# Column sums of phi(k) from operand sums, z placed later, and reciprocals by Ln and Exp in a two-block linear-attention kernel

## The chip, the cores and the metric

The kernel runs on one core of a Trainium2 chip. The metric is the device time of one execution in microseconds (us). Three runs of the kernel before gave 188.87, 189.10 and 189.14 us, median 189.1. The profile is of one further execution.

## The reference

```python
def _A_ref(x, wqkv, wo):                  # B=1, S=2048, D=640; _B_ref is the same function
    H = 32; Dh = D // H                   # 32 heads of 20
    q, k, v = ...                         # (x @ wqkv), split by kind and head
    phi = lambda t: jnp.where(t > 0, t + 1, jnp.exp(t)) + 1e-6
    pq, pk = phi(q), phi(k)
    kv = jnp.einsum("bhsd,bhse->bhde", pk, v)
    z = jnp.einsum("bhsd->bhd", pk)       # column sums of phi(k)
    num = jnp.einsum("bhqd,bhde->bhqe", pq, kv)
    den = jnp.einsum("bhqd,bhd->bhq", pq, z)[..., None] + 1e-6
    return merge_heads(num / den) @ wo

x = A_x
g = sigmoid((x * gate_w).sum(-1, keepdims=True))
a = _A_ref(x, A_wqkv, A_wo)
b = _B_ref(x, B_wqkv, B_wo)               # called on the same x
return g * a + (1 - g) * b
```

All arrays are bf16. Each token therefore needs, per head, one factor g/den for block A and (1-g)/den for block B.

## The kernel before

The 2048 tokens are 16 tiles of 128 (ST = 16, hc = 8 is half of them); the 640 features are 5 strips of 128 (DT = 5) or two halves of 320 (HF). `xn` holds x with tokens on partitions, `xT` with features on partitions. `pk` is phi(k) with tokens on partitions, `pqT[b]` is phi(q) with features on partitions, its features ordered so that partition p of strip m is feature 5p + m (`mixed`).

Instead of v, the kernel forms G = x^T phi(k), 640 by 640 (`GT`), then the per-head blocks of wv^T G, then M = (those blocks) wo. The output is the sum over both blocks of (scaled phi(q)) M.

**Stages, in PE's order.** k chunks and the first half of q of block A; then the second half of q (`q_pass`, five `q_unit`s, each two runs of five matmuls of 512 columns); then G of block A: the fifth strip of x plainly (`g_pass`, 32 matmuls of 320 columns), the other four strips by one level of Strassen's scheme (`g_strassen`, seven products of 16 matmuls, line 488). Block B's k and q follow, woven together (`q_strassen`), with M of A among them and after them (`m_block`, line 902). Then G of B in the same way (`g_pass`, `g_strassen`), M of B, and the output products over both blocks.

**Operand sums.** Strassen's scheme needs sums of quarters of x (`x_sum`, into `SX[1..4]`, VectorE, 128x2048) and of phi(k) (`k_sum`, into `TK[b][1..4]`, VectorE, 128x2560). b11, b12 are the first eight token tiles of phi(k), left and right half of the columns; b21, b22 are the last eight. All go through `add_rows` (line 627). For x transposed and wq the same is done by `sq_sum` and `tq_sums`; `p_diff` and `p_sums` make operands of the output products.

**The normalisation.** `z_rows` (line 551) multiplies a 128x32 block of ones with every token tile of `pk`: 16 tiles by two column halves, four tiles at a time on four 32-column strips of the PE array, and masks the result so that row h keeps only the 20 columns of head h (`zr`, line 556). `z_pass` (line 566) turns `zr` to features on partitions and adds the four strips, five matmuls of 32 columns, copied to `zsel` (line 570). `rec_pass` multiplies `zsel` with `pqT[b]` (line 203, 40 matmuls on 32-column strips): den, 32 heads by 4 token groups on partitions, 512 columns. Line 617 adds EPS and multiplies with the gate's factor `ge`, line 622 takes the reciprocal on VectorE. `norm_spread` (line 664) copies each head's row to its four partitions by eight matmuls of 32 rows, ScalarE writes `R` (line 669), and `scale` (line 677) multiplies `pqT[b]` with it.

The gate's logit comes as one more column of the first block's k product; `gl` is its Exp, `gate_rows` makes 1/g and 1/(1-g) of it (`gf`), `gate_spread` transposes them on PE (line 223), copies them (line 225) and sends them through DRAM to `ge` on SP's queue.

**What sets the order.** Under `manual_schedule` every engine executes its instructions in the order in which the program writes them; semaphores hold an instruction until its operands and its place are free. PSUM has four slots of two banks: `ps(name)` takes the next in turn, `ps(name, slot)` a named one, and a new tile in a slot waits for the last reader of the old one. So in `q_pass` the order is: unit 0, `z_rows`, `gate_spread`, then units with `x_sum` and `k_sum` in front of their phi on VectorE, `z_pass` after unit 2. In block B it is `g_pass` with two `m_block`s inside, `m_block` 2 and 3, `z_rows`, `m_block` 4 and 5, the reload of M through DRAM and the load of wo on SP, then `g_strassen` with `z_pass` in its first product.

Of the kernel before, what the change touches and what calls it, by code (L numbers as in the profile page):

```python
# [1 line left out]

# [6 lines left out]
P = 128  # L9
# [7 lines left out]
DT = D // P  # L17
# [7 lines left out]
NG = 8  # L25
K6 = 120
EPS = 1e-6
RB = 256
SH = S // 2

# [2 lines left out]
def kernel(  # L33
# [63 lines left out]
    spread = persist.tile([P, P], BF16, name="spread")  # L97
    R = persist.tile([P, 2, 4, RB], BF16, name="R")
    lift = persist.tile([P, 1], FP32, name="lift")
    ones = persist.tile([P, H], BF16, name="ones")  # L100
    g5 = persist.tile([DT, P], BF16, name="g5")
    gl = persist.tile([P, ST], FP32, name="gl")
# [30 lines left out]
    nc.vector.memset(ones[:], 1.0)  # L133
    nc.vector.memset(KVT[:], 0.0)
    nc.vector.memset(lift[:], 1.0 + EPS)
    xb0 = x2[0:CB * P, :].rearrange("(p q) d -> p q d", q=CB)
    wk = [None, None]
    wv = [None, None]
# [13 lines left out]
    load_x(nc.scalar, 2, 3)  # L152
    load_wk(nc.sync, 2, 3)
    load_x(nc.scalar, 3, 4)
    load_wk(nc.sync, 3, DT)
    wq[0] = wpool.tile([P, DT, D], BF16, tag="wq", name="wqA")
    for lo, hi in ((0, 2), (2, 4), (4, DT)):
# [166 lines left out]
    def mixed(t, m):  # L324

        return t[:, m::DT]
# [13 lines left out]
    def q_unit(b, m, h, lifted=False, slot=None, between=None):  # L340

        pt = ps(f"q{'AB'[b]}", slot)
        q_two(b, [(m, 2 * h), (m, 2 * h + 1)], pt)
        phi(pqT[b][:, m, h * 2 * HB:(h + 1) * 2 * HB].rearrange("p (b n) -> p b n", b=2), pt, lifted, between)

    def q_block(b, m, n, between=None):
# [100 lines left out]
    def g_pass(b, c, slot, between=None):  # L447

        pt = ps(f"g{'AB'[b]}", slot)
        for i in range(ST):  # L450
            if between is not None and i == ST // 2:
# [41 lines left out]
    def g_strassen(b, select, second, spare):  # L493

        x11, x12 = [xn[:, k:k + hc, 0:ic] for k in (0, hc)]
        x22 = xn[:, hc:ST, ic:2 * ic]
        b11 = pk[:, 0:hc, 0:HF]
        b21, b22 = [pk[:, hc:ST, n * HF:(n + 1) * HF] for n in range(2)]
        lo, hi = GT

        def temp(name):
            return work.tile([P, 2, HF], FP32, tag="osb", name=name, bufs=3)

        def add(dst, pt, sb):
# [5 lines left out]
        nc.scalar.copy(out=odd[:, :, 0:HF], in_=even[:, :, 0:HF])  # L510
        if b == 1:
# [4 lines left out]
        u2 = temp("u2")  # L516
        nc.scalar.copy(out=u2[:], in_=odd[:, :, 0:HF])
        if b == 1:
            k_sum(1, 4)
        g_prod(even, x12, b21, False)  # L520
        nc.scalar.copy(out=lo[:, 0:2, :], in_=even[:, :, 0:HF])
        if b == 0:
            k_sum(0, 4)
# [12 lines left out]
        scale(b, 2)  # L536
        scale(b, 3)
        g_prod(odd, x22, TK[b][4], False)
        nc.scalar.copy(out=lo[:, 2:4, :], in_=odd[:, :, 0:HF])
        scale(b, 4)  # L540
        g_prod(even, SX[4], b22, False)
        for n in range(2):
            nc.vector.tensor_tensor(out=hi[:, n, :], in0=even[:, n, 0:HF], in1=u2[:, n], op=ALU.add)

    def z_rows(b, slot=None):

        pt = ps(f"z{'AB'[b]}", slot)
        for k in range(ST // 4):
            for hf in range(2):
                for j in range(4):  # L550
                    nc.tensor.matmul(
                        pt[32 * j:32 * j + 32, hf, 0:HF], lhsT=ones[:], rhs=pk[:, 4 * k + j, hf * HF:(hf + 1) * HF],
                        start=(k == 0), stop=(k == ST // 4 - 1), tile_position=(0, 32 * j),
                    )
# [5 lines left out]
        return zr  # L560

    def z_pass(b, zr, slot=None):

        pt = ps(f"zs{'AB'[b]}", slot)
        for c in range(DT):
            nc.tensor.matmul(
                pt[:, 0, c * H:(c + 1) * H], lhsT=mixed(zr[:], c), rhs=I4[:], start=True, stop=True,
            )
        zsel = work.tile([P, DT, H], BF16, tag="zsel", name="zsel", bufs=1)
        nc.vector.tensor_copy(out=zsel[:], in_=pt[:, 0, 0:DT * H].rearrange("p (c h) -> p c h", h=H))  # L570
        return zsel

    def kvt_mm(b, pt, at, hf):
# [34 lines left out]
    def rec_pass(b, zsel, slot):  # L608

        pt = ps(f"den{'AB'[b]}", slot)  # L610
        for h in range(2):
            by_group(pt[:, 0, h * RB:(h + 1) * RB], zsel, pqT[b], h)
        rts = []
        for h in range(2):
            part = slice(h * RB, (h + 1) * RB)
            d1 = work.tile([P, RB], FP32, tag="d1", name="d1")
            nc.vector.scalar_tensor_tensor(
                out=d1[:], in0=pt[:, 0, part], scalar=EPS, in1=ge[:, b, part], op0=ALU.add, op1=ALU.mult
            )
            rT = work.tile([P, RB], BF16, tag="rT", name="rT")  # L620
            with nc.allow_low_precision(reason="a fp32 reciprocal, stored as the bf16 that multiplies bf16"):
                nc.vector.reciprocal(out=rT[:], in_=d1[:])
            rts.append(rT)
        return rts

# [152 lines left out]
    def q_pass(units):  # L778

        units = list(units)  # L780
        q_unit(0, *units.pop(0))
        zr = z_rows(0)
        gate_spread()
        for k in range(2):
            x_sum(1 + k)
            q_unit(0, *units.pop(0), True)
        zsel = z_pass(0, zr)
        for k, (m, h) in enumerate(units):
            if k < 2:
                if k:  # L790
                    x_sum(3)
                else:
                    k_sum(0, 2)
            q_unit(0, m, h, True)
        sq_sum(4, 0)
        return zsel

    with tc.manual_schedule():
        k_first()
# [19 lines left out]
    with tc.manual_schedule():  # L819
# [12 lines left out]
        g_strassen(0, lambda: zsel, 1, 3)  # L832

        tq_sums(1)
        new_stage("weave")
# [206 lines left out]
```

## Time and profile before

| What | us |
| --- | --- |
| median of three runs | 189.1 |
| the profiled execution | 189.34 |
| its span, first to last instruction | 187.6 |
| 38.5 to 58.3, second half of q, `g_pass` and first product of block A: PE / VectorE / ScalarE busy | 19.67 / 18.76 / 11.12 of 19.80 |
| 58.3 to 73.0, rest of `g_strassen` of A | 14.70 / 14.42 / 5.28 of 14.70 |
| 117.0 to 133.0, `g_pass` of B to `norm_spread` | 15.99 / 15.62 / 8.06 of 16.00 |
| 133.0 to 142.0, rest of `g_strassen` of B | 9.00 / 8.60 / 3.67 of 9.00 |

The profile names an instruction by its line, its engine, and out<-in with shapes. PE is TensorE's matmul and PEld its load of the stationary operand, which normally runs under the matmul before; `128*40` is such an operand of 128 rows and 40 columns, and `128x40` after it is the output. DVE is VectorE, ACT ScalarE, SP the queue that issues most DMA. A matmul's duration goes from its start to the arrival of its last column, so consecutive matmuls overlap; what one costs is the distance between starts. The chain of waits goes back from the last instruction, at each step to what released it; it is printed in order of time as start, length, what. Its times are those in which that link set the end.

The four reciprocals (line 622) take 1753 ns each, the column sums (line 551) 300 ns a matmul with four running side by side, and the table load of ScalarE (line 212) 1283 ns, once, at 2.69 us.

### The profile page before, as it was taken

How to read it: one execution, taken by the hardware profiler on the slowest of the kernel's cores; microseconds unless marked ns; L12 is line 12 of the kernel's file. 1: busy time of each engine (PE TensorE's matmuls, PEld its weight loads, DVE VectorE, ACT ScalarE, POOL GpSimd, SP SyncE). 2: the span in 40 equal slices, each digit the busy share in tenths (PEclk: the TensorE clock that was granted, in tenths of full speed). 3: DMA queues.
4: the chain of work that ended last, by engine and by line, in shares of the span. 5: the costliest groups of instructions: out<-in, count | busy, mean ns of one | idle time of the engine just before them, and what ended most of it. 6: DMA issues, size and time to landing. Idle time of an engine off the chain costs nothing.

```text
span 187.6 us, 3635 instructions
## 1 busy us (share of the span) xinstructions
PE 182.6 (97%) x1447; PEld 122.5 (65%) x1456; DVE 155.8 (83%) x268; ACT 87.0 (46%) x150; POOL 9.1 (5%) x25
## 2 busy tenths in 40 slices
PE   8899999999999999999999999999999999999993
PEld 3666657765577677676666655767677776777772
DVE  1468868889999999998898987999997989787554
ACT  2065488545842432455868686662611611111110
POOL 8920000000000000000000000000000000000000
PEclk9999999999999999999999999999999999999999
DMA  5996449984250000005000000145600003312222
GB/s 181 277 171 86 101 98 302 349 205 152 56 178 0 0 3 0 0 3 175 0 0 5 0 0 0 34 141 198 159 0 0 3 0 104 109 70 71 73 72 70
DMA packets 19769, 16.18 MB, mean 86 GB/s; under 512 B 8968, under 2 KB 19624, under 8 KB 19752
## 3 DMA queue, kind: packets, MB, share of 16 engines
q1 hardware_dynamic: 18888, 15.13, 29.3%
q10 hardware_dynamic: 864, 0.82, 1.3%
q8 instruction: 11, 0.18, 0.4%
q14 instruction: 6, 0.05, 0.1%
HBM read 10.52 MB, written 3.46 MB: 74 GB/s over the span
## 4 chain that ended last, share of the span: by engine, by line
PE 90%; DMA 4%; DVE 3%; issue 1%; ACT 1%; DVEq 0%; ACTq 0%
PE gs L488 17%; PE qA L329 11%; PE kB L277 11%; PE kA L277 10%; PE q L383 7%; PE ox L688 6%; PE oy L688 5%; PE oz L688 5%; DMA wkA<-in_A_wqkv_dram 3%; PE ow L688 3%; PE gB L459 2%; PE gA L459 2%; DMA xn<-in_A_x_dram 2%; PE qB L329 1%; PE q L329 1%; DVE osb L693 1%
## 5 line engine op out<-in xcount | busy, mean ns | idle before, releaser
L277 PEld LDWEIGHTS <-xT 128*128 128x128 bf16 x320 | 31.0, 97 | 15.2 <-issue 1.0
L256 DVE TENSOR_SCALAR e<-e 128x640 bf16<-128x640 bf16 (+2 forms) x56 | 19.4, 346 | 7.9 <-ACT e L251 7.4
L277 PE MATMUL kB<-wkB,xT 128*128 128x320 bf16 x160 | 24.2, 299 | 0.0
L277 PE MATMUL kA<-wkA,xT 128*128 128x320 bf16 (+1 forms) x160 | 23.0, 299 | 0.5 <-ACT wkA L212 0.3
L329 PE MATMUL qA<-xT,wqA 128*128 128x512 bf16 x96 | 22.4, 379 | 0.2
L329 PEld LDWEIGHTS <-wqA 128*128 128x128 bf16 x100 | 11.7, 118 | 9.2 <-issue 0.3
L251 ACT ACTIVATE e<-kA 128x640 bf16<-128x640 f32 x16 | 11.2, 706 | 10.1 <-PE kA L277 10.0
L488 PEld LDWEIGHTS <-xn 128*128 128x128 bf16 x128 | 12.2, 98 | 5.1 <-issue 0.3
L251 ACT ACTIVATE e<-kB 128x640 bf16<-128x640 f32 x16 | 11.3, 708 | 9.0 <-PE kB L277 8.9
L265 DVE SCALAR_TENSOR_TENSOR pk<-kA,e 128x640 bf16<-128x640 f32 x16 | 13.2, 825 | 2.1
L265 DVE SCALAR_TENSOR_TENSOR pk<-kB,e 128x640 bf16<-128x640 f32 x16 | 13.2, 824 | 1.5
L251 ACT ACTIVATE e<-qA 128x1024 bf16<-128x1024 f32 x10 | 10.2, 1023 | 8.2 <-PE qA L329 7.9
L732 ACT COPY u<-ox 128x320 f32<-128x320 f32 x8 | 3.4, 425 | 21.6 <-PE ox L688 21.6
L251 ACT ACTIVATE e<-q 128x512 bf16<-128x512 f32 x18 | 10.8, 597 | 5.4 <-PE q L383 3.8
L688 PEld LDWEIGHTS <-xT 128*128 128x128 bf16 x85 | 8.0, 98 | 3.1 <-DVE xT L627 0.2
L688 PEld LDWEIGHTS <-pqTA 128*128 128x128 bf16 x85 | 7.9, 98 | 2.9 <-issue 0.2
L688 PEld LDWEIGHTS <-pqTB 128*128 128x128 bf16 x80 | 7.8, 98 | 3.0
L693 DVE TENSOR_TENSOR osb<-oz,u 128x320 bf16<-128x320 f32 (+1 forms) x18 | 8.0, 453 | 2.0 <-PE oz L688 0.9
L383 PE MATMUL q<-xT,wqB 128*128 128x512 bf16 x32 | 9.5, 379 | 0.0
L488 PE MATMUL gs<-pk,xn 128*128 128x320 bf16 x64 | 9.5, 299 | 0.0
L459 PEld LDWEIGHTS <-xn 128*128 128x128 bf16 x64 | 6.3, 98 | 3.0 <-issue 0.4
L716 ACT COPY p1s<-ox 128x320 f32<-128x320 f32 x8 | 3.4, 425 | 10.3 <-PE ox L688 10.3
(150 smaller groups left out, 319.2 us busy)
## 6 DMA issues: line engine op xcount, KB each, us to landing
out_dram<-osb SPq DMA_DIRECT2D x14, 160.0 KB, 1.9
xn<-in_A_x_dram SPq DMA_DIRECT2D x3, 640.0 KB, 5.7
wvA<-in_A_wqkv_dram SPq DMA_DIRECT2D x1, 800.0 KB
wkB<-in_B_wqkv_dram SPq DMA_DIRECT2D x1, 800.0 KB, 4.8
wqB<-in_B_wqkv_dram SPq DMA_DIRECT2D x1, 800.0 KB, 4.8
wvB<-in_B_wqkv_dram SPq DMA_DIRECT2D x1, 800.0 KB
MA<-m_rows SPq DMA_DIRECT2D x1, 800.0 KB, 4.5
woB<-in_B_wo_dram SPq DMA_DIRECT2D x1, 800.0 KB
```

Of the source, the lines that this page charges most:

```text
L251: nc.scalar.activation(out=to, in_=part, func=ACT.Exp)
L256: nc.vector.tensor_scalar(self.e, self.e, 1.0, EPS, op0=ALU.min, op1=ALU.add)
L265: nc.vector.scalar_tensor_tensor(out=dst, in0=src, scalar=1.0 + EPS, in1=e, op0=ALU.add, op1=ALU.max)
L277: nc.tensor.matmul(pt[:, hf, 0:n], lhsT=xT[:, c, i * P:(i + 1) * P], rhs=wk[b][:, c, hf * HF:hf * HF + n], start=(c == 0), stop=(c == DT - 1),
L329: nc.tensor.matmul(dst, lhsT=mixed(wq[b][:, c, :], m), rhs=xT[:, c, n * HB:(n + 1) * HB], start=first, stop=last,)
L383: nc.tensor.matmul(dst, lhsT=left(c), rhs=right(c), start=first and k == 0, stop=k == len(cs) - 1, skip_group_check=not first,)
L459: nc.tensor.matmul(pt[:, hf, 0:HF], lhsT=xn[:, i, c * P:(c + 1) * P], rhs=pk[:, i, hf * HF:(hf + 1) * HF], start=(i == 0), stop=(i == ST - 1),
L488: nc.tensor.matmul(pt[:, n, 0:HF], lhsT=left[:, i, n * P:(n + 1) * P], rhs=right[:, i, :], start=(first and i == 0), stop=(i == hc - 1), s ...
L688: nc.tensor.matmul(dst, lhsT=left[:, c, r0:r0 + P], rhs=right[:, c, :], start=(first and c == 0), stop=(c == DT - 1), skip_group_check=not ...
L693: nc.vector.tensor_tensor(out=dst, in0=acc, in1=sb, op=ALU.add)
L716: nc.scalar.copy(out=self.p1s[:], in_=self.at("x"))
L732: nc.scalar.copy(out=self.u2[:], in_=self.at("x"))
```

## The change

`k_sum` now builds T2 and T4 from T3 = b12 + b22: T2 = T3 - b11, T4 = b21 - T2 = b11 + b21 - T3; the signs of `SX[1..3]` follow. T3's column sums are z's right half, and those of T4 plus T3 are its left half. `z_rows` sums T3 and T4, eight tiles each: 16 matmuls instead of 32. `z_pass` adds T3's sums to the left half: after each of its five matmuls a second one, with 64 columns of `zr` as stationary operand and 16 moving columns, accumulates into the first 64 partitions of the same place. z shares one PSUM tile over both steps.

In block A `z_rows` moves behind the fifth q unit and `z_pass` into the last quarter of `g_pass`; `gate_spread` moves behind the second unit; T3, T2, T4 and `SX[1]` come in `q_pass`, `SX[2]` and `SX[3]` after `g_pass`, T1 after the reciprocals. In block B `z_rows` moves behind `g_strassen`'s first product, together with the last `m_block` and the two loads on SP, and `z_pass` into its second product; `rec_pass` follows that product.

The reciprocal of den times gate factor becomes Exp(-(Ln den + Ln factor)): ScalarE takes Ln of `gf` (128x32) once, and in each block Ln of two halves of den (128x256, with a bias column `tiny`) and Exp of the sums; VectorE adds in between. A scale LOGS keeps Ln's argument small. One table set that holds Exp and Ln is loaded in place of the old one.

```diff
+    nc.scalar.preload_act_table_set("natural_log_exp_and_others")
...
         nc.vector.tensor_scalar(gf[:], gf[:], 1.0, 1e30, op0=ALU.add, op1=ALU.min)
+        nc.scalar.activation(out=gf[:], in_=gf[:], func=ACT.Ln, scale=LOGS)
...
-            1: (x21, x22, ALU.add), 2: (SX[1], x11, ALU.subtract),
-            3: (x11, x21, ALU.subtract), 4: (x12, SX[2], ALU.subtract),
+            1: (x21, x22, ALU.subtract), 2: (x11, SX[1], ALU.subtract),
+            3: (x21, x11, ALU.subtract), 4: (x12, SX[2], ALU.subtract),
...
-        left, right = {1: lambda: (b12, b11), 2: lambda: (b22, t[1]), 3: lambda: (b22, b12), 4: lambda: (b21, t[2])}[k]()
-        add_rows(t[k], left, right, ALU.subtract)
+        left, right = {1: lambda: (b12, b11), 2: lambda: (t[3], b11), 3: lambda: (b22, b12), 4: lambda: (b21, t[2])}[k]()
+        add_rows(t[k], left, right, ALU.add if k == 3 else ALU.subtract)
...
-        g_prod(even, x11, b11, True, lambda: sel.append(select()))
+        g_prod(even, x11, b11, True, (lambda: sel.append(select())) if b == 0 else None)
         nc.scalar.copy(out=odd[:, :, 0:HF], in_=even[:, :, 0:HF])
         if b == 1:
-            for rows in part[1:4]:
-                p_diff(rows)
-        rts = rec_pass(b, sel[0], 2)
-        g_prod(odd, SX[2], TK[b][2], False)
+            m_block(5, 2)
+            nc.sync.dma_start(out=M[0][:], in_=m_rows[:].rearrange("(p m) d -> p m d", m=DT))
+            load_wo(1, nc.sync)
+            zr = z_rows(1, 1)
+            p_diff(part[0])
+        else:
+            rts = rec_pass(b, sel[0], 2)
+        g_prod(odd, SX[2], TK[b][2], False, (lambda: sel.append(z_pass(1, zr))) if b == 1 else None)
         u2 = temp("u2")
         nc.scalar.copy(out=u2[:], in_=odd[:, :, 0:HF])
         if b == 1:
-            k_sum(1, 4)
+            for rows in part[1:4]:
+                p_diff(rows)
+            rts = rec_pass(b, sel[0], 2)
+            k_sum(1, 1)
...
-        for k in range(ST // 4):
-            for hf in range(2):
+        for hf in (1, 0):
+            for k in range(hc // 4):
                 for j in range(4):
                     nc.tensor.matmul(
-                        pt[32 * j:32 * j + 32, hf, 0:HF], lhsT=ones[:], rhs=pk[:, 4 * k + j, hf * HF:(hf + 1) * HF],
+                        pt[32 * j:32 * j + 32, hf, 0:HF], lhsT=ones[:], rhs=TK[b][4 - hf][:, 4 * k + j, :],
...
         for c in range(DT):
+            at = HF + c * H
+            nc.tensor.matmul(pt[:, 0, at:at + H], lhsT=mixed(zr[:], c), rhs=I4[:], start=True, stop=True)
             nc.tensor.matmul(
-                pt[:, 0, c * H:(c + 1) * H], lhsT=mixed(zr[:], c), rhs=I4[:], start=True, stop=True,
+                pt[0:P // 2, 0, at:at + H // 2], lhsT=mixed(zr[:], c)[:, P // 2:P], rhs=I4[:, H // 2:H],
+                start=False, stop=True, skip_group_check=True,
             )
...
+            nc.scalar.activation(out=d1[:], in_=pt[:, 0, part], func=ACT.Ln, scale=LOGS, bias=tiny[:])
+            ds.append(d1)
+        for h, d1 in enumerate(ds):
             nc.vector.scalar_tensor_tensor(
-                out=d1[:], in0=pt[:, 0, part], scalar=EPS, in1=ge[:, b, part], op0=ALU.add, op1=ALU.mult
+                out=d1[:], in0=d1[:], scalar=-2.0 * math.log(LOGS), in1=ge[:, b, part], op0=ALU.add, op1=ALU.add
             )
-                nc.vector.reciprocal(out=rT[:], in_=d1[:])
+            nc.scalar.activation(out=rT[:], in_=d1[:], func=ACT.Exp, scale=-1.0)
...
         q_unit(0, *units.pop(0))
-        zr = z_rows(0)
-        gate_spread()
-        for k in range(2):
-            x_sum(1 + k)
+        for k in (2, 4):
+            k_sum(0, k)
             q_unit(0, *units.pop(0), True)
-        zsel = z_pass(0, zr)
+            if k == 2:
+                gate_spread()
+        zs = []
+        x_sum(1)
+        q_unit(0, *units.pop(0), True)
+        q_unit(0, *units.pop(0), True, behind=lambda: zs.append(z_rows(0)))
...
-        k_sum(0, 1)
-        zsel = q_pass([(m, 1) for m in range(DT)])
+        k_sum(0, 3)
+        zr = q_pass([(m, 1) for m in range(DT)])
         wq[1] = load_w(1, "q", nc.sync)
-        g_pass(0, DT - 1, 1)
-        k_sum(0, 3)
+        zsel = []
+        g_pass(0, DT - 1, 3, lambda: zsel.append(z_pass(0, zr)), ST - CB)
+        x_sum(2)
+        x_sum(3)
...
-        for k in (1, 2, 3):
+        for k in (3, 2, 4):
             k_sum(1, k)
...
         m_block(2, 2)
         m_block(3, 3)
-        zr = z_rows(1, 1)
-        m_block(4, 2)
-        m_block(5, 3)
-        nc.sync.dma_start(out=M[0][:], in_=m_rows[:].rearrange("(p m) d -> p m d", m=DT))
-        load_wo(1, nc.sync)
+        m_block(4, 1)
-        p_diff(part[0])
-        g_strassen(1, lambda: z_pass(1, zr, 1), 3, 1)
+        g_strassen(1, None, 3, 1)
```

More of the change, by code (lines that the diff above doesn't have):

```diff
@@ L1 @@
+import math
 from contextlib import ExitStack
@@ L27 @@
 EPS = 1e-6
+LOGS = 2.0 ** -44
 RB = 256
@@ L99 @@
     lift = persist.tile([P, 1], FP32, name="lift")
+    tiny = persist.tile([P, 1], FP32, name="tiny")
     ones = persist.tile([P, H], BF16, name="ones")
@@ L135 @@
     nc.vector.memset(lift[:], 1.0 + EPS)
+    nc.vector.memset(tiny[:], LOGS * EPS)
     xb0 = x2[0:CB * P, :].rearrange("(p q) d -> p q d", q=CB)
@@ L338, in q_two, with q_unit @@
             q_mm(b, *parts[u], c, pt[:, u, :], c == 0, c == DT - 1)
-    def q_unit(b, m, h, lifted=False, slot=None, between=None):
+    def q_unit(b, m, h, lifted=False, slot=None, between=None, behind=None):
         pt = ps(f"q{'AB'[b]}", slot)
         q_two(b, [(m, 2 * h), (m, 2 * h + 1)], pt)
+        if behind is not None:
+            behind()
         phi(pqT[b][:, m, h * 2 * HB:(h + 1) * 2 * HB].rearrange("p (b n) -> p b n", b=2), pt, lifted, between)
@@ L445, in evac, with g_pass @@
         copy(out=dst.rearrange("p (b n) -> p b n", b=2), in_=pt[:, :, 0:HF])
-    def g_pass(b, c, slot, between=None):
+    def g_pass(b, c, slot, between=None, at=ST // 2):
         pt = ps(f"g{'AB'[b]}", slot)
         for i in range(ST):
-            if between is not None and i == ST // 2:
+            if between is not None and i == at:
                 between()
@@ L522, in g_strassen @@
         if b == 0:
-            k_sum(0, 4)
+            k_sum(0, 1)
             x_sum(4)
@@ L559, in z_rows, with z_pass @@
         )
-        return zr
-    def z_pass(b, zr, slot=None):
-        pt = ps(f"zs{'AB'[b]}", slot)
+        return pt, zr
+    def z_pass(b, zr):
+        pt, zr = zr
         for c in range(DT):
+            at = HF + c * H
+            nc.tensor.matmul(pt[:, 0, at:at + H], lhsT=mixed(zr[:], c), rhs=I4[:], start=True, stop=True)
             nc.tensor.matmul(
-                pt[:, 0, c * H:(c + 1) * H], lhsT=mixed(zr[:], c), rhs=I4[:], start=True, stop=True,
+                pt[0:P // 2, 0, at:at + H // 2], lhsT=mixed(zr[:], c)[:, P // 2:P], rhs=I4[:, H // 2:H],
+                start=False, stop=True, skip_group_check=True,
             )
         zsel = work.tile([P, DT, H], BF16, tag="zsel", name="zsel", bufs=1)
-        nc.vector.tensor_copy(out=zsel[:], in_=pt[:, 0, 0:DT * H].rearrange("p (c h) -> p c h", h=H))
+        nc.vector.tensor_copy(out=zsel[:], in_=pt[:, 0, HF:HF + DT * H].rearrange("p (c h) -> p c h", h=H))
         return zsel
@@ L612, in rec_pass @@
             by_group(pt[:, 0, h * RB:(h + 1) * RB], zsel, pqT[b], h)
-        rts = []
+        rts, ds = [], []
         for h in range(2):
@@ L616, in rec_pass @@
             d1 = work.tile([P, RB], FP32, tag="d1", name="d1")
+            nc.scalar.activation(out=d1[:], in_=pt[:, 0, part], func=ACT.Ln, scale=LOGS, bias=tiny[:])
+            ds.append(d1)
+        for h, d1 in enumerate(ds):
+            part = slice(h * RB, (h + 1) * RB)
             nc.vector.scalar_tensor_tensor(
-                out=d1[:], in0=pt[:, 0, part], scalar=EPS, in1=ge[:, b, part], op0=ALU.add, op1=ALU.mult
+                out=d1[:], in0=d1[:], scalar=-2.0 * math.log(LOGS), in1=ge[:, b, part], op0=ALU.add, op1=ALU.add
             )
             rT = work.tile([P, RB], BF16, tag="rT", name="rT")
-            with nc.allow_low_precision(reason="a fp32 reciprocal, stored as the bf16 that multiplies bf16"):
-                nc.vector.reciprocal(out=rT[:], in_=d1[:])
+            nc.scalar.activation(out=rT[:], in_=d1[:], func=ACT.Exp, scale=-1.0)
             rts.append(rT)
@@ L781, in q_pass @@
         q_unit(0, *units.pop(0))
-        zr = z_rows(0)
-        gate_spread()
-        for k in range(2):
-            x_sum(1 + k)
+        for k in (2, 4):
+            k_sum(0, k)
             q_unit(0, *units.pop(0), True)
-        zsel = z_pass(0, zr)
[L788 to L794, printed above, removed]
+            if k == 2:
[4 more added lines that the diff above has]
+        q_unit(0, *units.pop(0), True, behind=lambda: zs.append(z_rows(0)))
+        zr = zs[0]
         sq_sum(4, 0)
-        return zsel
+        return zr
     with tc.manual_schedule():
```

10 lines of the change are left out of this document (5 added, 5 removed).

## The prediction, made before any run of the changed kernel

> "Block A" and "block B" are the two attention blocks; line numbers are those of the kernel before.
>
> **What bounds the kernel now.** I read the busy row of each engine first, then the chain of work that ended last, then narrow stretches of the timeline.
>
> ```profile
> PE 182.6 (97%) x1447; PEld 122.5 (65%) x1456; DVE 155.8 (83%) x268; ACT 87.0 (46%) x150; POOL 9.1 (5%) x25
> PE   8899999999999999999999999999999999999993
> ```
>
> TensorE (PE) is busy in every slice between the first load and the last store. The chain says the same: 90% of it is PE, and in the two stretches that the edits touch, from 41 to 73 us in A and from 117 to 142 us in B, it never leaves PE. So a microsecond of PE time saved or added there is a microsecond of the end. VectorE and ScalarE count only if they make PE wait.
>
> ```profile
> 44.62 0.38 PE qA L329
> 45.00 0.03 issue
> 45.02 2.32 PE qA L329 x10
> 47.34 0.17 PE zsA L566 x5
> ...
> 122.61 1.20 PE zB L551 x32
> 123.81 0.79 PE mA L902 x4
> 124.60 1.19 PE gs L488 x8
> 125.79 0.17 PE zsB L566 x5
> ```
>
> The reader sees what the edits touch: 32 column-sum matmuls take 1.20 us of the path (L551), the five that turn them into zsel 0.17 us (L566). The four reciprocals on VectorE (1.75 us each) are nowhere on it.
>
> The price that decides is in the timeline: what PE loses between matmuls that use the whole array and matmuls that use a narrow strip of it.
>
> ```profile
> 84.42 0.19 PEld L875 LDWEIGHTS <-wvA 128*40 128x40 bf16 x5
> 84.65 0.11 PEld L383 LDWEIGHTS <-MB 128*128 128x128 bf16 x2
> ```
>
> ```profile
> 84.47 0.25 PE L875 MATMUL kvA<-GT,wvA 128*40 128x40 bf16 x4
> ```
>
> ```profile
> 5.34 0.09 PEld L211 LDWEIGHTS <-g 5*128 5x128 bf16 x1 [0.26 <-issue]
> 5.34 0.17 PE L211 MATMUL warm<-ident,g 5*128 5x5 bf16 x1
> 5.44 0.10 PEld L277 LDWEIGHTS <-xT 128*128 128x128 bf16 x1
> ```
>
> Columns: start, time, engine, line. The 40-column matmuls of L875 last 0.18 us each (row of L875), so the last of the four, ending at 84.72, began at 84.54. The next weights are those of a 128-column matmul, and they start only at 84.65: 0.11 us later, of which the 40 columns stream 0.017 us (L488: 320 columns every 0.136 us, from 16 in 2.17 us of the chain). So **a change between full width and a strip costs 0.09 us**, in which no weights are loaded ahead. The 5x5 matmul, narrow in rows, shows it for a tiny matmul: 0.10 us from its weights to the next. The same 0.09 us lies before and after L551, L203 and L664.
>
> **The change, part by part.**
>
> *Column sums (L551).* 32 matmuls in groups of four, one group every (1.27 - 0.30)/7 = 0.14 us (32 last 1.27 us, one lasts 0.30). 16 fewer are four groups: -0.55 us a block, **-1.10 us**.
>
> *zsel (L566).* Five full matmuls of 32 columns become ten: each is followed by one with 64 columns of weights and 16 moving columns. The compiled program gives the new ones a 128 by 64 part of the array, as it gives L875's 40-column ones, and the old ones the whole. So the width changes at every one, ten times a block, the way out included. A full one: weights 0.04 us (five in 0.19 us, from 47.18 to 47.37), streaming 0.014, change 0.09: 0.145 us; the first finds its weights loaded, 0.104. A narrow one: weights 0.02 (half as many columns; L875's five take 0.10 us), streaming 0.007, change 0.09: 0.12 us. Sum 0.104 + 4 x 0.145 + 5 x 0.12 = 1.28 us, where 0.19 us stood: +1.09 us a block, **+2.18 us**. Bounds: the smallest change that I find is 0.07 (gt at 42.55 to qA at 42.68, less 0.053 of streaming), the largest 0.10; the narrow weights lie between 0.017 and 0.04. That is 1.7 to 2.6 us.
>
> In two sentences that the rest can do without: the Trainium skill, TensorE: Matmul & The Clock Gate, section "Single matmul latency", gives a matmul that overlaps nothing (398 + N)/2.4 ns, 0.18 us at 32 columns, and if every change waited for such a whole matmul the ten would be near 2 us. The row at 84.65, 0.11 us after a start, is against it, and I go by the row.
>
> *Other changes of width.* In A the gate's transpose (L223), until now next to the sums, stands alone among full matmuls: one change more, +0.10. In B the order mA, sums, mA, 40-row mA, gs (L902) becomes mA, gs, 40-row mA, sums, gs: one change less (-0.09), and mA no longer loads 120 columns cold (-0.05). Together **-0.04 us**.
>
> *A wait goes.* In A, PE starts at 45.02 where 44.62 + 0.22 = 44.84 was due: it waited for VectorE's top of the first q unit (43.75 + 1.23 = 44.98), late behind k_sum, whose bank it reuses. The sums no longer take a turn of the four banks, so the unit that waits for this bank is the fourth, due at 45.8: **-0.19 us**.
>
> *A wait comes.* In B g_strassen's first matmul needs slot 0, which ScalarE empties with the two GT copies (122.10 + 0.75 = 122.85, 0.05 to be seen). The sums stood between. Now six mA matmuls of 0.136 from 121.90 end at 122.72: **+0.18 us** (bounds 0 to 0.25).
>
> *Work moved on VectorE and ScalarE* (times on the clock of before, each block for itself). In A the sums need T3 (done 43.31) and T4. Walking VectorE's new order with the old durations (T 1.49, clamp 0.42, top 0.69, x_sum 1.22, zr 0.82) T4 is ready at 49.0; PE arrives after five units, at 50.2. zr is ready at 53.2, z_pass comes at 54.1. SX[2] is ready near 57.0, needed at 60.0. ScalarE's Ln of gf comes ahead of the first Exp and holds it till 42.15; that Exp was to wait for T3 on VectorE anyway. The gate's row copy and its five DMA on SP come some 2.7 us later (43.16 to about 45.8) and land about 50, for a use at 60; SP's next load, wqB, isn't needed before 74. In B zr is ready at 127.15 and z_pass comes at 127.26, the narrowest place: a late zr costs up to 0.1. MA's reload follows the last mA store, 1 us later, landing 132.9 for TM0 at 133.9; woB follows it, for a use at 144.8.
>
> *Reciprocals.* VectorE's four of 1.75 us go. Ln and Exp of 128x256 aren't in the trace. Neighbours: 128x512 0.60 without bias, 0.69 with a bias column, 128x1024 1.02 and 1.11; so 0.82 ns a column, and 0.39 (Exp) and 0.48 (Ln); bounds 0.25 (COPY 32x128) and 0.69. I take 0.39 and 0.48: in B den ends near 131.1, Ln to 132.0, VectorE's adds (0.39) to 132.45, Exp to 132.9. L664 wants the first at 133.2, the second at 133.3. What VectorE wins it can't use: the scaling behind waits for R from ScalarE (134.0 + 1.94 in B), which waits for PE. Cost 0 with 0.3 us to spare; all at 0.69 they come 0.3 us late. One table load of 1.28 us stays where it was, before the first copy.
>
> **Sum**: -1.10 + 2.18 - 0.04 - 0.19 + 0.18 = +1.03 us. The profiled execution took 189.34 (span 187.6, so 1.7 around it), 0.24 above the median 189.1. Added to its own time: 190.4; to the median: **190.1 us**. With all bounds together +0.4 to +1.6; its own range is 189.5 to 190.7.
>
> **Rivals.**
> - *The 64-column matmuls cost no change of width* (the array takes them among full ones as it takes L577's 80 columns, where the trace shows no gap). Then ten small ones cost 5 x 0.04 + 5 x 0.025 = 0.33 us, +0.14 a block: -1.10 + 0.28 - 0.04 - 0.19 + 0.18 = -0.87, **188.2 us**, faster. It decides as soon as a change costs under 0.04 us. For: 16 matmuls really go. Against: L875 shows 0.09 us.
> - *Every change waits for the whole matmul.* They last 0.188 (L566) and 0.182 (L875's 40 columns); with weights 5 x 0.228 + 5 x 0.202 - 0.04 = 2.11 us, +1.92 a block: +2.7, **191.8 us**. Against: in L211's lines the next weights start at 5.44, before that matmul ends at 5.51. This is the case of the Trainium skill's rule above.
> - *Ln, add, Exp come late for L664 in B*, at 0.69 each and two passages between engines more: +0.3 on top, **190.4 us**.
> - *The path has slack that I don't see* (a wait for a bank later, 0.15 us before kB at 78.03 or 0.29 us before gB at 117.01, takes in the delay): at most 0.44 us of A's share, and only if the late engine isn't itself behind PE, which it is in both; near **189.5** with the sum's low bounds, about within 0.2% of before.
>
> **Chances.** Forecast 0.66, no change of width 0.14, whole matmul 0.05, late reciprocals 0.09, slack 0.06. A difference under 0.2%, 0.38 us, can't be told from none. The forecast's low end is just above that, the first rival is faster, the last the same: faster 0.15, same 0.08, slower 0.77. The range 189.1 to 190.9 holds forecast, late reciprocals and slack; the two ends are left out.
>
> **What would show it.** In the trace after: sums of 0.7 us instead of 1.27; ten zs matmuls over 1.2 to 1.3 us with starts 0.10 to 0.15 apart (step two; 0.3 us would prove the first rival, 2 us the second); no PE gap in the fourth q unit; gs waiting some 0.2 us for ScalarE's GT copy in B; L664's line without a wait for Exp. PE's total should rise by about 1 us with VectorE's falling by some 6. The forecast is wrong if the ten stand closer than 0.06 us.

## The result, and the profile after

The changed kernel took 190.56 us (median of six runs, 190.36 to 190.80) beside 189.15 for the kernel before on the same chip (six runs, 188.87 to 189.82): ratio 1.0069, 95% interval 1.0050 to 1.0087, slower by 0.5 to 0.9%. The profiled execution took 190.45 us, its span 188.7.

Spans carry the start-up with them: the first unit of the second half of q (`qA`, 39.10 us in the trace before) begins anywhere between 38.42 and 39.23 us in the traces of this study, and nothing ahead of it takes part in the change's steps on PE. So all traces are compared from that matmul to the last instruction: the **path** from here on.

| trace | path | block A, that matmul to `exA` | block B, `gB` to `exB` |
| --- | --- | --- | --- |
| before | 187.63 - 39.10 = 148.53 | 24.87 | 15.64 |
| after | 188.71 - 38.63 = 150.08 | 25.49 | 16.50 |

The path grew by 1.55 us, 0.62 of it in A and 0.86 in B; the stretches between and behind them differ by 0.06 at most, 0.07 together. The busy row of the page after:

```profile
PE 183.9 (97%) x1426; PEld 123.9 (66%) x1434; DVE 149.2 (79%) x265; ACT 90.1 (48%) x159; POOL 9.1 (5%) x25
```

PE rose by 1.3 us with 21 matmuls fewer in the records, and VectorE's work fell by 6.6. The chain of waits of the kernel after, block A (start, length, what):

```profile
49.70 0.66 PE zA L566 x16
50.35 3.37 PE gA L467 x24
53.72 0.02 PE zA L582
53.73 0.17 PE zA L583
53.90 0.14 PE zA L582
54.05 0.17 PE zA L583
...
54.99 0.17 PE zA L583
55.16 1.19 PE gA L467 x8
```

The sums (L566, formerly L551) hold the path for 0.66 us where they held it for 1.20: what the edit was to win. But the ten zsel matmuls (L582 full width, L583 narrow) follow each other every 0.14 and 0.17 us where five took 0.17 in all. The timeline of the same kernel shows why:

```profile
53.55 0.18 PE L582 MATMUL zA<-I,zr 128*128 128x32 bf16 x1
53.66 0.15 PEld L583 LDWEIGHTS <-zr 128*64 128x64 bf16 x1
53.66 0.24 PE L583 MATMUL zA<-I,zr 128*64 128x16 bf16 x1
53.83 0.12 PEld L582 LDWEIGHTS <-zr 128*128 128x128 bf16 x1
53.84 0.21 PE L582 MATMUL zA<-I,zr 128*128 128x32 bf16 x1
53.98 0.15 PEld L583 LDWEIGHTS <-zr 128*64 128x64 bf16 x1
```

The first of the ten finds its weights loaded (at 53.42, not shown). The weights (PEld) of every later one start 0.11 to 0.17 us after the matmul before it: 53.66, 53.83, 53.98. None is loaded ahead. From the first of the ten to the next `gA` matmul 1.54 us pass (53.55 to 55.09), and as much in B, where 0.19 stood before.

Most other steps are as forecast. In A no gap is left in the q units, as this row of the same chain shows: 30 matmuls of 512 columns in 6.47 us, 0.216 each.

```profile
43.22 6.47 PE qA L335 x30
```

In B `gs` waits for the GT copies on ScalarE (timeline, then chain, after):

```profile
122.27 0.75 ACT L464 CAST GT<-gB 128x320 bf16<-128x320 f32 x2 [1.16 <-PE gB L467]
```

```profile
122.23 0.82 PE mA L922 x6
123.05 0.02 issue
123.07 2.33 PE gs L496 x16
```

The copies end at 123.02 and `gs` starts at 123.07, with 0.187 us of PE lost in front of it. And the reciprocals are in time:

```profile
131.52 0.84 ACT L635 ACTIVATE d<-denB,tiny 128x256 f32<-128x256 f32 x2 [0.47 <-PE denB L208]
132.03 0.79 DVE L639 SCALAR_TENSOR_TENSOR d<-d,ge 128x256 f32<-128x256 f32 x2 [0.39 <-ACT d L635]
132.49 0.78 ACT L643 ACTIVATE rT<-d 128x256 bf16<-128x256 f32 x2
133.68 0.40 PE L685 MATMUL exB<-rT,spread 32*128 32x256 bf16 x8
```

The last Exp ends at 133.27, 0.41 us before L685 (formerly L664) starts on `rT`, and L685's line shows no wait. Of single instructions of 128x256, an Ln takes 0.47 us, an Exp 0.42 and an add 0.43.

### The profile page after: what moved, and what is told of

It reads as the page before. It is cut to its first block, busy times and chain, and to the rows that moved or that the text cites. A ratio compares the mean times of both kernels' runs of the same rounds, so it can differ in the third digit from the quotient of the medians.

```text
span 188.7 us, 3594 instructions
## 1 busy us (share of the span) xinstructions
PE 183.9 (97%) x1426; PEld 123.9 (66%) x1434; DVE 149.2 (79%) x265; ACT 90.1 (48%) x159; POOL 9.1 (5%) x25
## 4 chain that ended last, share of the span: by engine, by line
PE 94%; DVE 2%; ACT 1%; issue 1%; DVEq 0%; ACTq 0%
PE gs L496 17%; PE kA L283 12%; PE qA L335 11%; PE kB L283 11%; PE q L391 7%; PE ox L709 6%; PE oy L709 5%; PE oz L709 5%; PE ow L709 3%; PE gA L467 2%; PE gB L467 2%; PE warm L201 2%; PE qB L335 1%; PE q L335 1%; DVE osb L714 1%; PE kvA L895 1%
## 5 line engine op out<-in xcount | busy, mean ns | idle before, releaser
L496 PEld LDWEIGHTS <-xn 128*128 128x128 bf16 x128 | 12.3, 98 | 5.4 <-issue 0.9
L698 DVE TENSOR_TENSOR pqTA<-pqTA,R 128x2048 bf16<-128x2048 bf16 x5 | 5.8, 1219 | 3.2 <-ACT R L690 3.2
```

Of the source, the lines that this page charges most:

```text
L496: nc.tensor.matmul(pt[:, n, 0:HF], lhsT=left[:, i, n * P:(n + 1) * P], rhs=right[:, i, :], start=(first and i == 0), stop=(i == hc - 1), s ...
L698: nc.vector.tensor_tensor(out=pqT[b][:, m, :], in0=pqT[b][:, m, :], in1=rec, op=ALU.mult)
```

## The experiments

The theory, W (for width): the changes of width between the ten zsel matmuls cost the time, and all else comes out near nothing. Its rivals: a narrow matmul is dear whatever stands beside it (S), or the later place with its new waits costs the time, or the Ln/Exp do (V). After the first results a smaller question was added: why a narrow matmul holds the path for 0.172 us where the sum had 0.12.

### Five full, then five narrow

```diff
             nc.tensor.matmul(pt[:, 0, at:at + H], lhsT=mixed(zr[:], c), rhs=I4[:], start=True, stop=True)
+        for c in range(DT):
+            at = HF + c * H
             nc.tensor.matmul(
                 pt[0:P // 2, 0, at:at + H // 2], lhsT=mixed(zr[:], c)[:, P // 2:P], ...
```

> The changed kernel, but zsel's five full matmuls come first and its five 64-column ones behind them: two changes of width a block in place of ten. Theory W (the changed kernel loses its time to changes of width, and its zsel step takes 1.54 us a block): the step falls to 4 x 0.04 + 0.10 for the full ones, 0.075 + 4 x (0.025 to 0.075) for the narrow ones and 0.10 for the way out, 0.54 to 0.74 us, so 0.8 to 1.0 us less a block and 188.6 to 189.0 us in all. Rival S (a 64-column matmul costs 0.17 us whatever stands beside it): the step takes about 1.05 us, 189.6 us in all. Rival V (the time is lost in waits on the later z and on Ln and Exp): no change, 190.5 us.

Measured: 188.85 us, ratio to before 0.999 (0.9977 to 1.0002). The same ten matmuls on the same data, with two changes of width instead of ten. The timeline, block A:

```profile
53.34 0.34 PE L582 MATMUL zA<-I,zr 128*128 128x32 bf16 x5
53.61 0.54 PE L585 MATMUL zA<-I,zr 128*64 128x16 bf16 x5
54.09 0.58 PE L467 MATMUL gA<-pk,xn 128*128 128x320 bf16 x3
```

The step takes 0.75 us (53.34 to 54.09) instead of 1.54, twice 0.79 less, and the path is 148.48, 1.60 shorter than after. Order alone does that, and rival S, which asked for 189.6 us, falls. The five narrow ones still stand 0.076 us apart among themselves, without a change between them: that part is their own.

### All ten at full width

`zr` goes into the place of `KVT`, followed by 64 columns of zeros, so that the second matmul of each pair can take 128 columns too:

```diff
+    zpad = KVT[:].rearrange("p a b c -> p (a b c)")
...
-                pt[0:P // 2, 0, at:at + H // 2], lhsT=mixed(zr[:], c)[:, P // 2:P], rhs=I4[:, H // 2:H],
+                pt[:, 0, at:at + H // 2], lhsT=mixed(zpad[:, HF:HF + D], c), rhs=I4[:, H // 2:H],
```

> The changed kernel with all ten zsel matmuls at full width: the second of each pair takes the same 128-column view of zr, moved by 320 columns, with zeros behind the end (zr lies in KVT's place, whose zeros GpSimd restores in block B). Theory W: ten matmuls 0.04 us apart, 0.40 us a block where 1.54 stood, so 2.3 us less, 188.3 us, which is 0.8 us under the kernel before. Rival S: the same. Rival V: the step gets shorter, the waits stay, 190.5 us.

Measured: 188.11 us, ratio 0.9951 (0.9933 to 0.9969): faster than both kernels. Timeline, block A:

```profile
53.82 0.18 PE L581 MATMUL zA<-I,KVT 128*128 128x32 bf16 x1
53.85 0.18 PE L582 MATMUL zA<-I,KVT 128*128 128x16 bf16 x1
53.89 0.19 PE L581 MATMUL zA<-I,KVT 128*128 128x32 bf16 x1
...
54.20 0.57 PE L468 MATMUL gA<-pk,xn 128*128 128x320 bf16 x3
```

0.039 us apart, 0.38 us in all: 1.16 less in each block. 150.08 - 2.32 = 147.76, and the path is 147.77. A matmul twice as wide as needed costs less than a quarter of a narrow one that stands among full ones (0.039 against 0.172).

### The reciprocals back on VectorE

The Ln of `gf` goes too; the cut shows the rest.

```diff
-            nc.scalar.activation(out=d1[:], in_=pt[:, 0, part], func=ACT.Ln, scale=LOGS, bias=tiny[:])
...
-                out=d1[:], in0=d1[:], scalar=-2.0 * math.log(LOGS), in1=ge[:, b, part], op0=ALU.add, op1=ALU.add
+                out=d1[:], in0=pt[:, 0, part], scalar=EPS, in1=ge[:, b, part], op0=ALU.add, op1=ALU.mult
...
-            nc.scalar.activation(out=rT[:], in_=d1[:], func=ACT.Exp, scale=-1.0)
+                nc.vector.reciprocal(out=rT[:], in_=d1[:])
```

> The changed kernel with the four reciprocals on VectorE again and no Ln or Exp of them. Theory W: Ln and Exp cost nothing and pay for the later z: with 1.75 us each the second reciprocal ends about 64.7 us in block A, 0.4 us after PE wants it, and about 135.9 us in block B, 2.2 us after: 2.6 us more, 193.1 us (1.5 to 4 more). Rival V: this is the part that cost, so 190 us or less.

Measured: 193.63 us, ratio 1.0248 (1.0215 to 1.0280). Timeline, block B (the bracket is the idle time in front and what ended it):

```profile
133.16 1.75 DVE L639 RECIPROCAL rT<-d 128x256 bf16<-128x256 f32 x1
135.22 1.75 DVE L639 RECIPROCAL rT<-d 128x256 bf16<-128x256 f32 x1
135.24 0.29 PE L681 MATMUL exB<-rT,spread 32*128 32x256 bf16 x4 [0.35 <-DVE d L634]
137.03 0.29 PE L681 MATMUL exB<-rT,spread 32*128 32x256 bf16 x4 [1.50 <-DVE rT L639]
```

With z so late, two reciprocals in a row end at 136.97, and PE stands still for 1.50 us before it can use the second. Ln and Exp win no time against the kernel before; they pay for the later z, whose price without them would be 2.6 us of path (152.68 against 150.08; 0.23 of it is lost in a place that the last two runs look at).

### Ln and Exp in the kernel before

The same lines as above, put into the kernel before, and nothing else.

> The kernel before with Ln, add and Exp in place of the four reciprocals and nothing else changed. Theory W: the reciprocals are off the path there, so no change, 189.15 us, within 0.3 us. Rival V (Ln and Exp cost on ScalarE): 189.5 us or more. A third view (VectorE's 7 us of reciprocals did hold something up): 188.7 us or less.

Measured: 189.15 us, ratio 1.0004 (0.9991 to 1.0017), path 148.58: nothing either way.

### The placing alone

The kernel after, with the sums as before (32 matmuls from phi(k)) and five zsel matmuls:

```diff
-            for k in range(hc // 4):
+            for k in range(ST // 4):
...
-                        pt[32 * j:32 * j + 32, hf, 0:HF], lhsT=ones[:], rhs=TK[b][4 - hf][:, 4 * k + j, :],
+                        pt[32 * j:32 * j + 32, hf, 0:HF], lhsT=ones[:], rhs=pk[:, 4 * k + j, hf * HF:(hf + 1) * HF],
...
-            nc.tensor.matmul(
-                pt[0:P // 2, 0, at:at + H // 2], lhsT=mixed(zr[:], c)[:, P // 2:P], rhs=I4[:, H // 2:H],
-                start=False, stop=True, skip_group_check=True,
-            )
```

> The changed kernel with the column sums taken as before (32 matmuls from phi(k), both halves) and zsel by five full-width matmuls, without the narrow ones; the later places of both steps, the new order of the operand sums and the reciprocals by Ln and Exp stay. By theory W (widths): the zsel step falls from 1.53 to about 0.19 us a block, -2.68 us; the sums go back up, +1.10: 190.56 - 2.68 + 1.10 = 189.0 us, within 0.2 us of the kernel before. Rival 'placing' (the later z, its new waits and the Ln/Exp are what costs, the narrow matmuls only look dear): the time stays above 190 us. Against the version with all ten at full width (188.11) this gives the halved sums alone: 0.7 to 0.9 us.

Measured: 188.93 us, ratio 0.9992 (0.9979 to 1.0005). Its chain has the rows of the kernel before, at the places of the kernel after:

```profile
49.74 1.20 PE zA L566 x32
...
54.30 0.17 PE zA L582 x5
...
124.99 1.20 PE zB L566 x32
...
127.38 0.17 PE zB L582 x5
```

Path 148.43: the new places, waits, operand order and Ln/Exp together are worth -0.10 us. The rival 'placing' asked for over 190 us and falls. By A and B it is -0.19 and +0.04, which are the forecast's wait that goes (-0.19) and the wait that comes less the change of width and the cold weights (+0.18 - 0.14). Against the full-width version the halved sums are worth 148.43 - 147.77 = 0.66 us; the rows give -1.08 for the sums and +0.39 for five matmuls more in each block, -0.69. By path the expectation's 0.7 to 0.9 was a little high.

### Why the narrow weights are slow: zr strip by strip

`mixed` takes every fifth column of `zr`. Here `zr` is stored strip by strip, so that the columns of a matmul lie side by side:

```diff
-        zr = work.tile([P, D], BF16, tag="zr", name="zr", bufs=1)
+        zr = work.tile([P, DT, P], BF16, tag="zr", name="zr", bufs=1)
+        for hf in range(2):
+            nc.vector.tensor_tensor(
+                out=zr[:, :, hf * (P // 2):(hf + 1) * (P // 2)].rearrange("p c m -> p m c"), ...
```

> The changed kernel with zr stored strip by strip, so that the stationary columns of the ten zsel matmuls lie side by side instead of five elements apart; their order and widths stay (full, narrow, full, narrow ...). VectorE writes zr in two instructions instead of one. In the changed kernel a narrow matmul holds the path for 0.172 us where the sum had 0.12, that is 0.075 us for its weights where 0.02 was taken. Theory 'stride' (the spacing of the columns makes the narrow load slow): the narrow load falls to 0.03 us, the full one from 0.04 to 0.03, so a pair falls from 0.314 to about 0.26 us, 0.27 us a block, 0.55 in all: 190.0 us. Rival 'strip' (a load into the 64-column part takes 0.075 us wherever its columns lie): only the full ones gain, 0.01 each, 0.1 us in all: 190.5 us. Either way the 0.09 us of every change stays. If zr takes VectorE longer in two instructions, block B's zsel step waits for it, up to 0.3 us, to be seen as a gap before its first matmul.

Measured: 194.34 us (median of six, 193.21 to 196.64), ratio 1.0271 (1.0222 to 1.0320), a miss in time. The instructions on the tile `zr` (shortest, median and longest in ns), first of the kernel after, then of this one:

```profile
L582 PEld LDWEIGHTS <-zr x10: 117/118/118, 53.4 to 128.7; 128*128 128x128 bf16 x10
L583 PEld LDWEIGHTS <-zr x10: 148/148/150, 53.7 to 128.8; 128*64 128x64 bf16 x10
L571 DVE TENSOR_TENSOR zr<-zA,E x1: 817/817/817, 51.8 to 51.8; 128x640 bf16<-128x640 f32 x1
```

```profile
L584 PEld LDWEIGHTS <-zr x10: 95/96/96, 54.8 to 133.4; 128*128 128x128 bf16 x10
L585 PEld LDWEIGHTS <-zr x10: 106/106/106, 54.9 to 133.5; 128*64 128x64 bf16 x10
L572 DVE TENSOR_TENSOR zr<-zA,E x2: 1577/1690/1802, 51.8 to 53.0; 128x320 bf16<-128x320 f32 x2
```

On PE the theory 'stride' holds: the narrow load shortens by 0.042 us, the full one by 0.022, and a pair takes 0.249 us (0.120 for the full matmul, 0.129 for the narrow one) instead of 0.314. For columns side by side the forecast's 0.12 us for a narrow matmul was 0.01 short. But VectorE now writes single elements 256 bytes apart and needs 3.4 us for what took 0.82, and PE waits for `zr`. Timeline, block A:

```profile
54.82 0.19 PE L584 MATMUL zA<-I,zr 128*128 128x32 bf16 x1 [1.09 <-DVE zr L572]
```

The bracket counts from the end of the matmul before; from start to start it is 1.385 us where 0.136 is usual, a wait of 1.25 us. In B it is 2.08.

The same layout with full width (strips of 192 columns in the place of `KVT`, the last 64 zero):

```diff
-                pt[:, 0, at:at + H // 2], lhsT=mixed(zpad[:, HF:HF + D], c), rhs=I4[:, H // 2:H],
+                pt[:, 0, at:at + H // 2], lhsT=zpad[:, c, P // 2:P // 2 + P], rhs=I4[:, H // 2:H],
```

> All ten zsel matmuls at full width as in the version that took 188.11 us, with the stationary columns side by side (strips of 192 columns, the last 64 zero). There the ten stood 0.039 us apart, weights 0.04 us each. Theory 'stride': the ten stand about 0.027 us apart, the step falls from 0.38 to 0.26 us a block: 187.9 us. Rival: the load of 128 columns takes 0.04 us wherever the columns lie: 188.1 us, or up to 0.3 us more where VectorE's zr in two instructions comes late in block B.

Measured: 191.74 us, ratio 1.0158 (1.0133 to 1.0183). The ten stand 0.025 us apart (0.027 by the theory 'stride'), and the same two waits for VectorE, 1.25 and 2.08 us, outweigh it; in time this is a miss too.

### Read with a stride, write side by side

Only the order of the elements in VectorE's two instructions is turned round, and their own order (right half first); at full width, and in the same way with alternating widths:

```diff
-                out=zpad[:, :, hf * (P // 2):(hf + 1) * (P // 2)].rearrange("p c m -> p m c"),
-                in0=pt[:, hf, 0:HF].rearrange("p (m c) -> p m c", c=DT), ...
+                out=zpad[:, :, hf * (P // 2):(hf + 1) * (P // 2)],
+                in0=pt[:, hf, 0:HF].rearrange("p (m c) -> p c m", c=DT), ...
```

> The version with all ten zsel matmuls at full width and their stationary columns side by side, as before, but VectorE now reads the sums with a stride and writes zr side by side (the last one wrote with a stride: 1.58 to 1.80 us for half of zr, 2.08 us of waiting in block B). If the stride of the writes was dear, each half takes VectorE some 0.45 us (0.82 for both in one instruction in the changed kernel), zr comes in time, the ten stand 0.026 us apart, and the step falls by 0.13 us a block against the 0.039 us apart of the version that took 188.11: 187.85 us. Rival: any stride on one side costs the same, zr takes 3.4 us again and the time is 191.7 us. In between: zr some 0.1 to 0.2 us late in block B, 188.0 us.

> The changed kernel (alternating widths) with the stationary columns of zr side by side, VectorE reading with a stride and writing side by side. On PE the pair of a full and a narrow matmul took 0.249 us with columns side by side and 0.314 with columns five elements apart, so five pairs in two blocks save 0.65 us when zr comes in time: 190.56 - 0.65 = 189.9 us. Rival: the strided read makes zr as late as the strided write did, over 193 us.

> The version with all ten zsel matmuls at full width, stationary columns five elements apart, once more, beside the gathered one on the same chip: 188.1 us as before.

Measured on one chip, beside 188.93 us for the kernel before:

| version | us | ratio | path |
| --- | --- | --- | --- |
| full width, gathered | 188.28 | 0.9963 (0.9949 to 0.9977) | 147.76 |
| alternating, gathered | 190.34 | 1.0062 (1.0044 to 1.0080) | 149.72 |
| full width, spaced columns, again | 188.40 | 0.9969 (0.9954 to 0.9983) | 147.76 |

All three are above what was expected (187.85, 189.9 and 188.1). Half of `zr` takes 0.52 us now and comes in time, at worst 0.02 us late. The alternating version gains 0.31 us up to `exA` and 0.27 in B, as the pairs said, but its path is only 0.36 shorter than that of the kernel after; the full-width one should have gained 0.25 us over the spaced one and gains nothing. The rest goes in a place that the edits don't touch: from the first k product of B to its first G product the four versions with two VectorE instructions for `zr` take 44.25 or 44.26 us; before, after, the grouped, the full-width version and the placing alone take 44.01 to 44.03.

### One instruction more

Two runs for that: the gathered version with one instruction for `zr`, and the spaced one with an idle instruction more.

```diff
-        for hf in (1, 0):
-            nc.vector.tensor_tensor(out=zpad[:, :, hf * (P // 2):(hf + 1) * (P // 2)], ...
+        nc.vector.tensor_tensor(
+            out=zpad[:, :, 0:P].rearrange("p c (b m) -> p b c m", b=2), ...
```

```diff
+        spare = work.tile([P, 1], FP32, tag="spare", name="spare", bufs=1)
+        nc.vector.memset(spare[:], 0.0)
         nc.vector.tensor_tensor(
             out=zpad[:, 0:D].rearrange("p (b n) -> p b n", b=2), in0=pt[:, :, 0:HF],
```

> The gathered version at full width (zr read with a stride, columns side by side) with one VectorE instruction for zr instead of two. In the four versions with two instructions, block B from its first k product to its first product of G took 44.25 us instead of 44.02, because one VectorE multiply into phi(q) began 0.34 us after its input; the versions with one instruction don't show it. Theory 'count' (one VectorE instruction more in front of it does it): 44.02 us again, and the whole gain of the closer columns, 0.26 us, against the full-width version with spaced columns: ratio to before 0.9955 or below. Rival 'layout' (the place or shape of zr does it): 44.25 us again, ratio 0.996 to 0.997.

> The version at full width with spaced columns, and one VectorE instruction more in each block ahead of zr (a column of zeros that nobody reads, some 0.06 us). Theory 'count': the late multiply appears here too, the stretch from the first k product of block B to its first product of G takes 44.25 us instead of 44.02, and the time rises by 0.2 to 0.3 us. Rival 'layout': 44.02 us, the time of the version without it, up to 0.1 us more.

Measured: 188.16 us, ratio 0.9950 (0.9933 to 0.9967), that stretch 44.03, path 147.53, the shortest of all; and 188.45, ratio 0.9974 (0.9957 to 0.9992), that stretch 44.26, path 147.98. So it is the count and not the layout; the intervals of the times alone, 0.9974 beside 0.9951 and 0.9969 without the idle instruction, would not show it. Timeline of the full-width version, then of the one with the idle instruction:

```profile
98.07 0.70 ACT L260 ACTIVATE pqTB<-q,lift 128x512 bf16<-128x512 f32 x1
98.81 0.69 DVE L267 TENSOR_TENSOR pqTB<-pqTB,e 128x1024 bf16<-128x1024 bf16 x1 [0.15 <-ACT pqTB L260]
```

```profile
98.40 0.70 ACT L260 ACTIVATE pqTB<-q,lift 128x512 bf16<-128x512 f32 x1
99.45 0.69 DVE L267 TENSOR_TENSOR pqTB<-pqTB,e 128x1024 bf16<-128x1024 bf16 x1 [0.48 <-ACT pqTB L260]
```

The multiply starts 0.03 us behind its input in the first and 0.36 in the second, for one 128x1 instruction 47 us earlier. The kernel after with the reciprocals on VectorE, two instructions more in block A, shows the 44.26 us as well. Counted in the traces with VectorE's semaphore instructions, the multiply is the 191st record in the eight traces where it is on time, that of the kernel before among them, and the 192nd in the six where it is late. So what counts is its place in the engine's order. What holds it there isn't settled: in every trace a packet of a queue of kind "instruction" starts 0.7 to 1.0 us behind it, late or not, which neither shows a load of code nor rules it out.

## Why the prediction was right, and where it wasn't

The side, the range (189.1 to 190.9) and the mechanism were right; the sum was +1.03 us and the path shows +1.55. By its steps:

- *Column sums, -0.55 a block*: 0.66 against 1.20 us in the chain, -0.54. Right.
- *zsel, +1.09 a block*: 1.54 against 0.19, +1.35. This is the **mis-sized term**, 0.26 us a block, 0.5 in all. Its full matmul (0.145, measured 0.142) holds, and so does its change of width: 0.142 less 0.04 for weights and 0.014 of streaming leaves 0.09, and 0.172 less 0.076 (the spacing of the grouped narrow ones) and 0.007 leaves 0.09 too. The narrow matmul was 0.172 instead of 0.12, for its weights take some 0.075 us and not 0.02. The 0.02 was half of the full one's 0.04, backed by L875, whose weights lie side by side while those of `zr` lie five elements apart; the bounds, 0.017 to 0.04, didn't hold 0.075 either. Five times 0.052 is the 0.26. With columns side by side the narrow one came down to 0.129. That spaced narrow weights take longer than spaced full ones, no row of before showed.
- *Other changes of width, -0.04*: the term of gt alone, +0.10, didn't come. In the trace after, gt's weights are loaded ahead (at 42.73, gt starts at 42.95) and the next matmul starts 0.11 us behind it, so it shows no change of width in front. A's ledger is -0.55 + 1.35 - 0.19 = 0.61 without it, and 0.62 is measured. In B it is -0.55 + 1.35 - 0.14 + 0.18 = 0.84 against 0.86.
- *The wait that goes in A (-0.19) and the one that comes in B (+0.18)*: no gap in the fourth q unit, and 0.187 us before `gs`. Right.
- *Work moved*: nothing moved to VectorE, ScalarE or SP came late; with the placing alone the path changed by -0.10, all of it told by the waits and the change of width.
- *Reciprocals, 0 with 0.3 us to spare*: 0.41 to spare; in the kernel before they change nothing. Right, and without them the later z would cost 2.6 us.
- *Sum and base*: 1.03 + 0.52 - 0.10 = 1.45 of the 1.55 measured; 0.07 of the rest lies in the stretches outside A's and B's steps and isn't explained. The medians differ by 1.41, the profiled times by 1.11, for the start-up of the profiled execution was 0.47 us shorter after. The zsel term, 2.70 us for both blocks, lies outside its own bounds (1.7 to 2.6). With gt's 0.10 as forecast the path would have grown by 1.65, past the bounds of the sum (+0.4 to +1.6): that these held is in part luck.

Of the rivals, 'no change of width' is refuted by the grouped order, which gives 1.6 us back and touches nothing else, and 'whole matmul' by starts 0.14 to 0.17 us apart instead of 0.20 to 0.23. 'Late Ln/Exp' is refuted by L685 without a wait, 'slack' by the path, which took the whole delay.

The Trainium skill, TensorEngine Tiling (Array Packing), section "Key Properties", says that a change of tiling mode drains TensorE, and gives no size. The ten matmuls fit that: 0.09 us each time, and 0.79 us a block less when eight of ten changes go (eight times 0.09, and the 0.08 of streaming that then runs under the next weights again).

## What to carry to other kernels

Here tiny matmuls on a narrow part of the array cost more by the changes between widths than by their size: give them the width of their neighbours, zeros and all (1.16 us a block here), or put those of one width together (0.79). A price taken from another row holds only for the same layout of the operand; look at the spacing of the stationary columns before borrowing it. Fewer matmuls are a gain only together with what has to put their results together: -1.08 us of sums was worth -0.66 with the cheap second step and +1.65 (150.08 against 148.43) with the dear one.

## What the runs showed of the hardware

- Spaced stationary columns (every fifth of bf16) cost more: between full-width matmuls of 32 and 16 columns 0.039 against 0.025 us. A 64-column operand on its part of the array takes 0.076 (narrow ones in a row) against some 0.03, an estimate: 0.129 from start to start less 0.09 for the change and 0.007 of streaming.
- VectorE takes 1.58 to 1.80 us for 128x320 when it writes bf16 elements 256 bytes apart, 0.50 to 0.53 when it reads five apart and writes side by side.
- A wait of PE can be followed by half the clock, and then costs more than itself. In the strip-by-strip version the stretches after the wait of 1.25 us read, with busy time of each engine, then the granted clock (0.54), DMA share and GB/s:

```profile
54.80:56.10 1.30, 1.28 (x11) 1.05 (x12) 1.20 (x3) 0.00 (x0) 0.00 (x0) 1.00 0.00 0
56.10:59.80 3.70, 3.70 (x17) 2.10 (x17) 3.67 (x6) 0.75 (x2) 0.00 (x0) 0.54 0.02 4
59.80:62.00 2.20, 2.20 (x47) 1.65 (x48) 1.64 (x3) 0.68 (x1) 0.00 (x0) 1.00 0.00 0
```

Matmuls of 320 columns stood 0.267 us apart there instead of 0.136: half the clock for some 3.4 us, from 1.3 us after the wait on. It came in some executions and not in others: three of the six of this version kept a granted clock of 0.999 or 1.0 and took 193.21 to 193.34 us. Its full-width sister shows the same wait of 1.25 us in A without it, and the kernel after with the reciprocals on VectorE waits 1.50 us in B without it. Which wait brings it isn't shown. The Trainium skill, TensorE: Matmul & The Clock Gate, section "Part 1: The HAM clock gate", gives half the clock after a window of 3.4 us without work; the length agrees, but here it came after only 1.25 us of waiting.
